# Pooled attention and a four-expert MLP on one core: queries by head pairs, low heads first, a new load order, and a re-ordered first chunk

## The chip, the cores and the metric

The kernel runs on one core of one Trainium2 chip. The metric is the device time of one execution in microseconds (us). The median of three runs of the kernel before is 489.83 us (489.71 to 490.68). One further execution was profiled; all rows below come from it.

The engines are named as in the profile: PE is TensorE (PEld its weight loads), DVE VectorE, ACT ScalarE, POOL GpSimd, SP SyncE. L12 is line 12 of the kernel before.

## The reference, cut to what matters

```
k_p = k.reshape(B, H, Sp, 8, D).mean(axis=3)      # B=8, H=8, S=576, D=64, Sp=72
v_p = v.reshape(B, H, Sp, 8, D).mean(axis=3)
attn = softmax(q @ k_p.T / sqrt(D));  x = attn @ v_p
x = x.transpose(0, 2, 1, 3).reshape(4608, 512)
p = domain_probs / domain_probs.sum(-1)
out = sum over e of p[:, e] * (relu(x @ w1[e]) @ w2[e])   # E=4, 512 -> 1024 -> 512
```

Attention over keys and values that are averaged eight by eight, then four experts of two layers, weighted by the given probabilities. Inputs and output are float32; the kernel computes in bfloat16 with float32 sums.

## The kernel before, in words

The 4608 tokens are worked on in nine chunks of 512: one for the first 512 tokens of each batch and one for the eight remainders of 64. A chunk and an expert are a step of the main loop. The two layers of an expert are not done as plain products but, in the main loop, in a seven-product scheme on half blocks (as in Strassen's method): `up_product` (L695) and `down` (L763) each make seven products per expert, with sums of weights (`weight_sums`, `first_weight_sums`), of inputs (`x_sum`) and of hidden values (`hidden_sums`), all by DVE at L246, in place of an eighth. `up` (L617), `up_quarter` (L631) and `down_plain` (L789) are plain products, used in the first chunk where the sums are not yet there.

All engines' orders are written out by hand (a manual schedule): the order of the calls is the order of the instructions on each engine, and semaphores are put in by the framework. So an instruction whose data is late holds everything behind it on its engine.

What the change touches:

- **The opening**, `attention_first`: batch 0's attention. `load_q` (L174) loads the queries as float32 in two halves of four heads, on SP's and ACT's queues; `round_q` (L186) casts a pair of heads to bfloat16 on DVE or ACT; `queries_first` (L364) turns a pair on PE and copies it back. Keys and values of batch 0 come by POOL's queue in four loads each (L142). They are pooled on PE: `choose_rows` and `rows_chosen` (L109, L110 on POOL and L246 on DVE) build a matrix of zeros and ones, `sum_keys` (L318) and `sum_values` (L306) multiply by it. `scores_first` (L545) with its exponential on ACT (L549), `context_quarter` (L440), the division on DVE (L429, L430) and `turn_quarter` (L455) follow for the low four heads (group 0) and the high four (group 1). `idle` (L338) issues matmuls on zeros: fillers, without a result that anyone reads.
- **The loads**: POOL's queue casts float32 to bfloat16 on the way. It brings, in the order of issue, batch 0's keys and values, the first layers of experts 0 to 2 with expert 0's second layer, expert 3's first layer, batch 1's keys (`load_whole`, L128, 72 partitions), batch 1's queries (L178), expert 1's second layer, batch 1's values in two loads, expert 2's second layer (`load_w2`, L216). Expert 3's second layer is issued from within `first_chunk`, since its buffer holds partial sums until then (`partial_first`).
- **The first chunk**, `first_chunk`: experts 0 to 3 on batch 0's tokens, with batch 1's attention in between. Here expert 0's and 1's first layers are plain; `both(e, step)` makes step `step` of the seven products for both units (halves of the hidden columns) of expert e. A unit has two PSUM banks. Step 0 fills bank 0, which ACT copies to bank 1 (L708); steps 2 and 3 add to bank 0, which ACT copies out after each (L710); step 1 and 6 add to bank 1, step 4 starts it anew and step 5 ends bank 0. ACT takes steps 1 and 5 (L712, L716), DVE steps 4 and 6 (L675). `down(c, e, step)` alternates between the two banks of `chains`; `down_plain(c, e, r)` uses `chains[r % 2]` for row block r, and its sum is added by DVE (L842). `fold_keys(1)` (L268, L286) and `values_folds(1)` (L268, L342) add up batch 1's eight rows on DVE; `queries_of_two` (L375, copy L378), `keys` (L297, copy L298), `scores_of_two` (L393), `context` (L467, L429, L430) and `turn` (L485, copy L486) are its attention.
- Behind `first_chunk` the **main loop** runs 7 x 32 slots, each with an up product of two units and a down step, and the next batch's pieces at planned slots. The change leaves it as it is.

The two functions that carry the order around the change are `attention_first` and `first_chunk`. The idle filler and the step that refills a bank, as written:

```
def idle(n, w_ps, cols=NT):
    for _ in range(n):
        nc.tensor.matmul(w_ps[:, 0:cols], lhsT=zeros[:, 0:P], rhs=zeros[:, 0:cols])
```

Of the kernel before, what the change touches and what calls it, by code (L numbers as in the profile page):

```python
# [17 lines left out]
def kernel(  # L18
# [10 lines left out]
    nc = tc.nc  # L29

    B, H, S, D = q.shape
    E, DM, F = moe_w1.shape
    P = nc.NUM_PARTITIONS
# [67 lines left out]

    ROWS = 9
# [96 lines left out]
    def load_w1(e):  # L199
        if e == 0:  # L200
            low, high = slice(0, HK), slice(HK, KC)
            parts = [(low, 0, 2), (high, 0, 2), (slice(0, KC), 2, 3), (slice(0, KC), 3, 4)]
        else:
            parts = [(slice(0, KC), 0, 4)] if e == E - 1 else [(slice(0, KC), 0, 2), (slice(0, KC), 2, 4)]
# [350 lines left out]
    def attention_first():  # L555
# [15 lines left out]
        sum_keys(0, (C0, C1))  # L571
        copy_keys(0, (C0, C1), (vector, scalar))
        idle(4, W2[:, 0], P)
# [21 lines left out]
        up_quarter(0, 1, (C0, C1))  # L595
        up_quarter(1, 1, (W2[:, 0], W2[:, 1]))
        for fc, bank in enumerate((B2[:, 0], A2[:, 0], C0, C1), HF):
            up(0, 0, (fc,), bank=bank)
# [274 lines left out]
    def first_chunk():  # L873
# [20 lines left out]
        each(sums[2][0], sums[2][1], sums[2][3], sums[2][2])  # L894
        up(0, 1, (5,), bank=chains[0])
        both(2, 0)
        up(0, 1, (6,), bank=chains[1])
        both(2, 1)
        up(0, 1, (7,), bank=chains[0])
        last_sum = weight_sums(0)  # L900
        each(sums[0][3], sums[1][3], *last_sum[0:2])
        both(2, 2)
        down(0, 0, 0)
        both(2, 3)
        hidden_sums(0, 0, 2)
        down(0, 0, 1)
        both(2, 4)
        hidden_sums(0, 0, 3)
        down(0, 0, 2)
        both(2, 5)  # L910
        each(*last_sum[2:])
        down(0, 0, 3)
        both(2, 6)
        each(*sums[3][0:2])
        both(3, 0)
        down(0, 0, 4)
        both(3, 1)
        each(sums[3][3], sums[3][2])
        fold_keys(1)
        down(0, 0, 5)  # L920
        both(3, 2)
        down(0, 0, 6)
        both(3, 3)
        queries_of_two(0, att[:, 0], nc.scalar.copy)
        both(3, 4)
        both(3, 5)
        keys(1, every)
        queries_of_two(2, chains[0][:], nc.scalar.copy)
        both(3, 6)
        load_w2(3)  # L930
        scores_of_two(1, 0, 0)
        down_plain(0, 1, 0)
        lo, hi = slice(0, H // 2), slice(H // 2, H)
        each(*values_folds(1, lo))
        scores_of_two(1, 2, 0)
        fold_first, *fold_rest = values_folds(1, hi)
        fold_first()
        down_plain(0, 1, 1)
        each(*fold_rest)
# [8 lines left out]
        down_plain(0, 1, 2)  # L948
        context(1, 0)
        down_plain(0, 1, 3)  # L950
# [3 lines left out]
        down_plain(0, 2, 0)  # L954
# [3 lines left out]
        down_plain(0, 2, 1)  # L958
# [3 lines left out]
        down_plain(0, 2, 2)  # L962
# [69 lines left out]
    with tc.manual_schedule(  # L1032
# [3 lines left out]
        load_first(k, "kraw", 1)  # L1036
        choose_rows()
        make_identity(nc, ident[:])
# [7 lines left out]
        rows_chosen(0)  # L1046
        rows_chosen(1)
# [79 lines left out]
```

## Time and profile before

| what | us |
|---|---|
| median of three runs | 489.83 |
| the profiled execution, own time | 489.93 |
| its span, first instruction to last | 488.2 |
| PE busy 0 to 6.4 / 6.4 to 17.7 | 4.90 / 10.17 |
| PE busy 17.7 to 50 (32.3 long) | 32.20 |
| PE busy 50 to 70.5 (20.5 long) | 19.87 |
| PE busy 70.5 to 488.2 (417.7 long) | 413.38 |
| ACT busy 50 to 70.5 | 8.46 |
| DVE busy 50 to 70.5 | 16.96 |
| busy share of the 16 DMA engines up to 70, in slices of 1.75 us | 0.9 or more in all but the first two |

How to read it: the span is what the trace covers; the execution's own time has 1.7 us around it. Busy PE counts pipelined matmuls whose ends are modelled, and they overlap, so a gap of 0.1 to 0.2 us between two matmuls does not show as idle. Whether PE lost time is read from the distance between the starts of neighbouring matmuls: eight 128x256 matmuls take 0.87 us in the chain, a 128x512 matmul 0.216 us from start to start, and anything above is a gap. For a group of instructions the timeline gives start, length and, in brackets, the idle time of the engine before it with what ended it.

### The profile page before, as it was taken

How to read it: one execution, taken by the hardware profiler on the slowest of the kernel's cores; microseconds unless marked ns; L12 is line 12 of the kernel's file. 1: busy time of each engine (PE TensorE's matmuls, PEld its weight loads, DVE VectorE, ACT ScalarE, POOL GpSimd, SP SyncE). 2: the span in 40 equal slices, each digit the busy share in tenths (PEclk: the TensorE clock that was granted, in tenths of full speed). 3: DMA queues.
4: the chain of work that ended last, by engine and by line, in shares of the span. 5: the costliest groups of instructions: out<-in, count | busy, mean ns of one | idle time of the engine just before them, and what ended most of it. 6: DMA issues, size and time to landing. Idle time of an engine off the chain costs nothing.

```text
span 488.2 us, 11522 instructions
## 1 busy us (share of the span) xinstructions
PE 480.5 (98%) x4673; PEld 409.4 (84%) x4678; DVE 376.9 (77%) x758; ACT 303.8 (62%) x576; POOL 119.4 (24%) x120
## 2 busy tenths in 40 slices
PE   8999999999999999999999999999999999999996
PEld 4669568898888888888888888888898888888885
DVE  4779799989768976798679866997678766876674
ACT  5677446855676567656765567556755567556650
POOL 8520504242523154016321442111011101010000
PEclk9999999999999999999999999999999999999999
DMA  9999999994986489345954298311111010004003
GB/s 195 203 209 203 204 170 155 103 90 54 110 110 63 77 86 137 35 83 56 159 50 91 27 165 66 68 23 66 35 23 23 23 64 3 12 23 87 1 1 87
DMA packets 104996, 41.96 MB, mean 86 GB/s; under 512 B 75504, under 2 KB 104432, under 8 KB 104944
## 3 DMA queue, kind: packets, MB, share of 16 engines
q0 software_dynamic: 58496, 22.35, 41.8%
q1 hardware_dynamic: 45328, 17.84, 16.7%
q10 hardware_dynamic: 1120, 1.05, 0.6%
q8 instruction: 36, 0.59, 0.5%
q14 instruction: 16, 0.13, 0.1%
HBM read 45.69 MB, written 9.44 MB: 113 GB/s over the span
## 4 chain that ended last, share of the span: by engine, by line
PE 91%; DMA 3%; ACT 2%; DVE 2%; POOL 1%; issue 1%; POOLq 0%; ACTq 0%
PE unit L695 42%; PE o_ps L763 41%; DMA w_bf<-in_moe_w_dram 3%; PE att L467 1%; PE unit L822 1%; PE o_ps L617 1%; PE att L393 1%; ACT expT L549 1%; PE unit L617 1%; PE unit L393 0%; DVE wt_bf L246 0%; POOL wt_bf L142 0%; ACT qT L378 0%; DVE acc L842 0%; PE work_first L631 0%
## 5 line engine op out<-in xcount | busy, mean ns | idle before, releaser
L842 DVE SCALAR_TENSOR_TENSOR acc<-o_ps,p_all,acc 128x256 f32<-128x256 f32 (+1 forms) x285 | 126.9, 485 | 52.9 <-PE o_ps L763 36.5
L763 PEld LDWEIGHTS <-H 128*128 128x128 bf16 x1320 | 129.1, 98 | 15.5 <-issue 0.6
L695 PEld LDWEIGHTS <-w_bf 128*128 128x128 bf16 x1088 | 105.2, 98 | 13.0 <-issue 0.2
L675 DVE CUSTOM_DVE_ANT_0 H<-unit,partial 128x512 bf16<-128x512 f32 x128 | 87.2, 684 | 23.8 <-ACT partial L710 11.5
L763 PE MATMUL o_ps<-w_bf,H 128*128 128x256 bf16 x792 | 102.6, 273 | 0.4 <-ACT o_ps L771 0.4
L695 PE MATMUL unit<-xT,w_bf 128*128 128x256 bf16 x704 | 100.5, 273 | 0.0
L777 POOL TENSOR_TENSOR acc<-acc,addend 128x512 f32<-128x512 f32 x24 | 30.7, 1279 | 253.2 <-ACT addend L775 202.2
L710 ACT COPY partial<-unit 128x512 f32<-128x512 f32 x128 | 72.3, 592 | 30.2 <-PE unit L695 30.2
L695 PEld LDWEIGHTS <-wu_bf 128*128 128x128 bf16 x816 | 77.6, 98 | 11.7 <-issue 2.5
L695 PE MATMUL unit<-xs,wu_bf 128*128 128x256 bf16 x512 | 77.0, 273 | 0.0
L763 PE MATMUL o_ps<-wt_bf,H 128*128 128x256 bf16 x528 | 68.4, 273 | 0.0
L712 ACT ACTIVATE H<-unit 128x512 bf16<-128x512 f32 x66 | 39.8, 605 | 30.9 <-PE unit L695 30.9
L763 PEld LDWEIGHTS <-S 128*128 128x128 bf16 x528 | 51.7, 98 | 6.0
L716 ACT ACTIVATE H<-unit 128x512 bf16<-128x512 f32 x66 | 39.6, 602 | 25.6 <-PE unit L695 25.3
L708 ACT COPY unit<-unit 128x512 f32<-128x512 f32 x68 | 39.4, 582 | 23.6 <-PE unit L695 18.0
L695 PE MATMUL unit<-xs,w_bf 128*128 128x256 bf16 x256 | 38.4, 273 | 0.0
L840 ACT ACTIVATE acc<-o_ps,p_all 128x256 f32<-128x256 f32 x72 | 30.7, 485 | 9.4 <-PE o_ps L763 7.7
L152 POOL DMA_DIRECT2D kraw<-in_k_dram x20 | 26.3, 1317 | 39.0 <-DMA kraw<-in_k_dram 39.0
L695 PE MATMUL unit<-xT,wu_bf 128*128 128x256 bf16 x240 | 35.7, 272 | 0.0
L763 PE MATMUL o_ps<-w_bf,S 128*128 128x256 bf16 x264 | 34.2, 273 | 0.0
L763 PE MATMUL o_ps<-wt_bf,S 128*128 128x256 bf16 x264 | 34.2, 273 | 0.0
L152 POOL DMA_DIRECT2D vraw<-in_v_dram x20 | 28.4, 1420 | 18.8 <-DMA vraw<-in_v_dram 18.5
(162 smaller groups left out, 500.2 us busy)
## 6 DMA issues: line engine op xcount, KB each, us to landing
out_dram<-acc SPq DMA_DIRECT2D x32, 256.0 KB, 4.2
w_bf<-in_moe_w_dram POOLq DMA_DIRECT2D x10, 512.0 KB, 17.4
q_sb<-in_q_dram POOLq DMA_DIRECT2D x7, 512.0 KB, 9.6
vraw<-in_v_dram POOLq DMA_DIRECT2D x22, 144.0 KB, 6.5
kraw<-in_k_dram POOLq DMA_DIRECT2D x21, 144.0 KB, 5.7
w_bf<-in_moe_w_dram POOLq DMA_DIRECT2D x2, 1024.0 KB, 17.8
w_bf<-in_moe_w_dram POOLq DMA_DIRECT2D x4, 256.0 KB, 7.3
wt_bf<-in_k_dram POOLq DMA_DIRECT2D x4, 144.0 KB, 5.4
```

What stands on the lines that cost most here:

```text
L152: nc.gpsimd.dma_start(out=raw[:], in_=rows_of(src, b, 2 * part, 2 * part + 2), accum_op=ALU.add if part else ALU.bypass)
L617: nc.tensor.matmul(out_ps, lhsT=w1_bf[:, e, kc, fc * P:(fc + 1) * P], rhs=xT[:, kc, at], start=(kc == 0), stop=(kc == KC - 1), skip_group_ ...
L675: nc.vector._custom_dve(TENSOR_ADD_SAT, out=dst, in0=ps, in1=part, s0=LARGEST, s1=0.0)
L695: nc.tensor.matmul(ps[:, n * HN:(n + 1) * HN], lhsT=lhs[:, kc, f:f + P], rhs=rhs[:, kc, :], start=(not grows and n == 0 and kc == 0), stop ...
L708: nc.scalar.copy(out=banks[1][:], in_=ps)
L710: nc.scalar.copy(out=part[:, step - 2], in_=ps)
L712: nc.scalar.activation(out=quarter(0, 0), in_=ps, func=ACT.Relu)
L716: nc.scalar.activation(out=quarter(0, 1), in_=ps, func=ACT.Relu)
L763: nc.tensor.matmul(ps[:, j], lhsT=lhs[:, i, j * P:(j + 1) * P], rhs=rhs[:, i, :], start=(not grows and i == 0 and j == 0), stop=(i == HF - 1),
L777: nc.gpsimd.tensor_add(out=dst, in0=dst, in1=addend[:])
L840: nc.scalar.activation(out=dst, in_=o_ps, func=ACT.Copy, scale=prob)
L842: nc.vector.scalar_tensor_tensor(out=dst, in0=o_ps, scalar=prob, in1=dst, op0=ALU.mult, op1=ALU.add,)
```

## The change

Queries of batch 0 are loaded in four loads of two heads, alternately on SP's and ACT's queues. The identity is built ahead of the row choice on POOL, and `rows_chosen` moves into `attention_first`. The opening's order changes: fillers 11 become 7 and are put differently (26 become 23 in all, of 512 or 128 columns); low keys are pooled ahead of the last query turn, the last turn's copy goes to DVE; both context quarters of the low heads come ahead of the second value pooling, and the last context quarter ahead of the first up product. Some results go to other PSUM banks.

`load_whole` splits the 72 partitions into 64 (in as many loads as before) and 8. `load_w1` cuts expert 1's first layer into a quarter, a quarter and a half of the hidden columns, and expert 2's by input rows (low half, high half) instead of by hidden columns. `load_w2(1)` moves ahead of batch 1's keys and queries.

In `first_chunk` the steps of expert 2 come earlier and closer together, expert 0's down steps follow with fewer products between them, expert 1's plain down products are cut into halves and start among expert 3's products, and batch 1's queries, keys, scores and contexts move behind expert 3's products.

```diff
@@ load_whole
+        rows = src[b].rearrange("h (j r) d -> j h r d", r=POOL)
         for i in range(n):
             hs = slice(i * H // n, (i + 1) * H // n)
-            nc.gpsimd.dma_start(
-                out=raw[:, hs], in_=src[b].rearrange("h (j r) d -> j h r d", r=POOL)[:, hs])
+            nc.gpsimd.dma_start(out=raw[0:EVEN, hs], in_=rows[0:EVEN, hs])
+        nc.gpsimd.dma_start(out=raw[EVEN:], in_=rows[EVEN:])
@@ load_q
-        for group, queue in enumerate((nc.sync, nc.scalar)):
-            hs = slice(4 * group, 4 * group + 4)
-            queue.dma_start(out=wide_q[:, hs], in_=src[:, hs])
+        for pair in range(NPAIR):
+            hs = slice(2 * pair, 2 * pair + 2)
+            (nc.sync, nc.scalar)[pair % 2].dma_start(out=wide_q[:, hs], in_=src[:, hs])
@@ load_w1
+            1: [(every, 0, 1), (every, 1, 2), (every, 2, 4)],
+            2: [(low, 0, 4), (high, 0, 4)],
@@ attention_first
-        idle(11, W2[:, 0])
+        idle(7, W2[:, 0])
         round_q(0, vector)
         round_q(1, scalar)
         queries_first((0,), C0, vector)
+        idle(1, W2[:, 0])
+        queries_first((1,), C1, scalar)
         round_q(2, vector)
         round_q(3, scalar)
-        idle(1, W2[:, 0])
-        queries_first((1,), C1, scalar)
-        idle(3, W2[:, 0], P)
+        rows_chosen(0)
+        rows_chosen(1)
         queries_first((2,), B2[:, 0], vector)
-        queries_first((3,), A2[:, 0], scalar)
-        idle(1, W2[:, 0])
-        sum_keys(0, (C0, C1))
-        copy_keys(0, (C0, C1), (vector, scalar))
-        idle(4, W2[:, 0], P)
+        idle(3, W2[:, 0])
+        sum_keys(0, (W2[:, 0], W2[:, 1]))
+        copy_keys(0, (W2[:, 0], W2[:, 1]), (vector, vector))
+        queries_first((3,), C1, vector)
+        idle(3, C0, P)
         scores_first(0, 0, B2)
         scores_first(0, 1, A2)
         sum_keys(1, (C0, C1))
         copy_keys(1, (C0, C1), (vector, vector))
-        idle(6, W2[:, 0], P)
+        idle(5, W2[:, 0], P)
         scores_first(1, 0, W2)
+        scores_first(1, 1, B2)
         sum_values(0, (C0, C1))
         cast_values(0, vector)
-        scores_first(1, 1, B2)
+        idle(4, A2[:, 0], P)
         context_quarter(0, 0, A2)
+        context_quarter(1, 0, W2)
         sum_values(1, (C0, C1))
         cast_values(1, scalar)
-        context_quarter(1, 0, W2)
         turn_quarter(0, 0, A2[:, 0], scalar)
         context_quarter(0, 1, B2)
-        turn_quarter(1, 0, W2[:, 0], scalar)
-        up_quarter(0, 0, (C0, C1))
-        context_quarter(1, 1, A2)
-        turn_quarter(0, 1, B2[:, 0], scalar)
-        up_quarter(1, 0, (W2[:, 0], W2[:, 1]))
-        turn_quarter(1, 1, A2[:, 0], vector)
+        turn_quarter(1, 0, C0, scalar)
+        context_quarter(1, 1, W2)
+        up_quarter(0, 0, (C1, A2[:, 0]))
+        turn_quarter(0, 1, C0, scalar)
+        up_quarter(1, 0, (B2[:, 0], B2[:, 1]))
+        turn_quarter(1, 1, W2[:, 0], vector)
...
@@ first_chunk, the new order from expert 1's up 5 on (the old one is in the listing above)
+        up(0, 1, (5,), bank=chains[0])
+        both(2, 0)
+        each(*sums[2][0:2], sums[2][3], sums[2][2])
+        up(0, 1, (6,), bank=chains[1])
+        up(0, 1, (7,), bank=chains[0])
+        both(2, 1)
+        both(2, 2)
+        last_sum = weight_sums(0)
+        each(sums[0][3], sums[1][3], last_sum[0])
+        both(2, 3)
+        down(0, 0, 0)
+        both(2, 4)
+        each(last_sum[1])
+        both(2, 5)
+        down(0, 0, 1)
+        hidden_sums(0, 0, 2)
+        both(2, 6)
+        down(0, 0, 2)
+        hidden_sums(0, 0, 3)
+        each(*last_sum[2:])
+        down(0, 0, 3)
+        down(0, 0, 4)
+        each(*sums[3][0:2])
+        both(3, 0)
+        down(0, 0, 5)
+        both(3, 1)
+        each(sums[3][3], sums[3][2])
+        down(0, 0, 6)
+        both(3, 2)
+        first, second = range(HF), range(HF, FCH)
+        down_plain(0, 1, 0, first)
+        both(3, 3)
+        down_plain(0, 1, 1, first)
+        both(3, 4)
+        down_plain(0, 1, 0, second)
+        fold_keys(1)
+        both(3, 5)
+        down_plain(0, 1, 1, second)
+        both(3, 6)
+        load_w2(3)
+        queries_of_two(0, att[:, 0], nc.scalar.copy)
+        queries_of_two(2, chains[1][:], nc.scalar.copy)
+        down_plain(0, 1, 2, first)
+        keys(1, every)
+        down_plain(0, 1, 2, second)
+        lo, hi = slice(0, H // 2), slice(H // 2, H)
+        each(*values_folds(1, lo))
+        scores_of_two(1, 0, 0)
+        down_plain(0, 1, 3)
+        each(*values_folds(1, hi))
+        scores_of_two(1, 2, 0)
+        down_plain(0, 2, 0, first)
+        down_plain(0, 2, 1, first)
...
         context(1, 0)
+        down_plain(0, 2, 0, second)
         context(1, 1)
         turn(1, 0)
         hidden_sums(0, 3, 0)
+        down_plain(0, 2, 1, second)
         context(1, 2)
         turn(1, 1)
         hidden_sums(0, 3, 1)
+        down_plain(0, 2, 2)
         context(1, 3)
         turn(1, 2)
         each(*weight_sums(3)[0:3])
-        down_plain(0, 2, 2)
         turn(1, 3)
         each(*(lambda n=n: x_sum(1, n) for n in range(3)))
@@ the opening calls
+        make_identity(nc, ident[:])
         choose_rows()
-        make_identity(nc, ident[:])
...
-        rows_chosen(0)
-        rows_chosen(1)
...
+        load_w2(1)
         load_whole(1, k, "kraw")
         load_q(1)
-        load_w2(1)
         load_whole(1, v, "vraw", 2)
```

More of the change, by code (lines that the diff above doesn't have):

```diff
@@ L99 @@
     raw_v = rawpool.tile([SP, H, 2, D], BF16, name="vraw")
+    EVEN = SP // 16 * 16
     ROWS = 9
@@ L199, in load_w1 @@
     def load_w1(e):
[L200 to L204, printed above, removed]
+        every, low, high = slice(0, KC), slice(0, HK), slice(HK, KC)
+        parts = {
+            0: [(low, 0, 2), (high, 0, 2), (every, 2, 3), (every, 3, 4)],
+            1: [(every, 0, 1), (every, 1, 2), (every, 2, 4)],
+            2: [(low, 0, 4), (high, 0, 4)],
+            3: [(every, 0, 4)],
+        }[e]
         for ks, lo, hi in parts:
@@ L577, in attention_first @@
         copy_keys(1, (C0, C1), (vector, vector))
-        idle(6, W2[:, 0], P)
+        idle(5, W2[:, 0], P)
         scores_first(1, 0, W2)
+        scores_first(1, 1, B2)
         sum_values(0, (C0, C1))
         cast_values(0, vector)
-        scores_first(1, 1, B2)
+        idle(4, A2[:, 0], P)
         context_quarter(0, 0, A2)
+        context_quarter(1, 0, W2)
         sum_values(1, (C0, C1))
         cast_values(1, scalar)
-        context_quarter(1, 0, W2)
         turn_quarter(0, 0, A2[:, 0], scalar)
         context_quarter(0, 1, B2)
-        turn_quarter(1, 0, W2[:, 0], scalar)
-        up_quarter(0, 0, (C0, C1))
-        context_quarter(1, 1, A2)
-        turn_quarter(0, 1, B2[:, 0], scalar)
-        up_quarter(1, 0, (W2[:, 0], W2[:, 1]))
-        turn_quarter(1, 1, A2[:, 0], vector)
-        up_quarter(0, 1, (C0, C1))
-        up_quarter(1, 1, (W2[:, 0], W2[:, 1]))
-        for fc, bank in enumerate((B2[:, 0], A2[:, 0], C0, C1), HF):
+        turn_quarter(1, 0, C0, scalar)
[4 more added lines that the diff above has]
+        turn_quarter(1, 1, W2[:, 0], vector)
+        up_quarter(0, 1, (C1, A2[:, 0]))
+        up_quarter(1, 1, (B2[:, 0], B2[:, 1]))
+        for fc, bank in enumerate((W2[:, 0], C0, C1, B2[:, 0]), HF):
             up(0, 0, (fc,), bank=bank)
@@ L893, in first_chunk @@
         up(0, 1, (4,), bank=units[0][1][:])
-        each(sums[2][0], sums[2][1], sums[2][3], sums[2][2])
         up(0, 1, (5,), bank=chains[0])
         both(2, 0)
+        each(*sums[2][0:2], sums[2][3], sums[2][2])
         up(0, 1, (6,), bank=chains[1])
+        up(0, 1, (7,), bank=chains[0])
         both(2, 1)
-        up(0, 1, (7,), bank=chains[0])
+        both(2, 2)
         last_sum = weight_sums(0)
-        each(sums[0][3], sums[1][3], *last_sum[0:2])
-        both(2, 2)
+        each(sums[0][3], sums[1][3], last_sum[0])
@@ L903, in first_chunk @@
+        both(2, 3)
         down(0, 0, 0)
-        both(2, 3)
+        both(2, 4)
+        each(last_sum[1])
+        both(2, 5)
+        down(0, 0, 1)
         hidden_sums(0, 0, 2)
-        down(0, 0, 1)
-        both(2, 4)
+        both(2, 6)
+        down(0, 0, 2)
         hidden_sums(0, 0, 3)
-        down(0, 0, 2)
-        both(2, 5)
         each(*last_sum[2:])
         down(0, 0, 3)
-        both(2, 6)
+        down(0, 0, 4)
         each(*sums[3][0:2])
         both(3, 0)
-        down(0, 0, 4)
+        down(0, 0, 5)
@@ L917, in first_chunk @@
         both(3, 1)
         each(sums[3][3], sums[3][2])
-        fold_keys(1)
[L920 to L925, printed above, removed]
+        down(0, 0, 6)
[6 more added lines that the diff above has]
+        down_plain(0, 1, 0, second)
+        fold_keys(1)
@@ L926, in first_chunk @@
         both(3, 5)
-        keys(1, every)
-        queries_of_two(2, chains[0][:], nc.scalar.copy)
+        down_plain(0, 1, 1, second)
         both(3, 6)
         load_w2(3)
-        scores_of_two(1, 0, 0)
-        down_plain(0, 1, 0)
+        queries_of_two(0, att[:, 0], nc.scalar.copy)
[3 more added lines that the diff above has]
+        down_plain(0, 1, 2, second)
         lo, hi = slice(0, H // 2), slice(H // 2, H)
@@ L934, in first_chunk @@
         each(*values_folds(1, lo))
+        scores_of_two(1, 0, 0)
+        down_plain(0, 1, 3)
+        each(*values_folds(1, hi))
         scores_of_two(1, 2, 0)
[L936 to L939, printed above, removed]
+        down_plain(0, 2, 0, first)
+        down_plain(0, 2, 1, first)
         load_wide(0, 0)
@@ L947, in first_chunk @@
         load_wide(1, 2)
-        down_plain(0, 1, 2)
         context(1, 0)
-        down_plain(0, 1, 3)
+        down_plain(0, 2, 0, second)
         context(1, 1)
@@ L953, in first_chunk @@
         hidden_sums(0, 3, 0)
-        down_plain(0, 2, 0)
+        down_plain(0, 2, 1, second)
         context(1, 2)
@@ L957, in first_chunk @@
         hidden_sums(0, 3, 1)
-        down_plain(0, 2, 1)
+        down_plain(0, 2, 2)
         context(1, 3)
```

## The prediction

> **What bounds the kernel now.** I read the page first, then the chain, the waits, and the timeline of the first 75 us. Times are us from the span's start; PE is TensorE, ACT ScalarE, DVE VectorE.
>
> ```profile
> PE 480.5 (98%) x4673; PEld 409.4 (84%) x4678; DVE 376.9 (77%) x758; ACT 303.8 (62%) x576; POOL 119.4 (24%) x120
> ...
> PE 91%; DMA 3%; ACT 2%; DVE 2%; POOL 1%; issue 1%; POOLq 0%; ACTq 0%
> ```
>
> PE does nearly all of the chain. The waits of PE from 65 us to the end are one line:
>
> ```profile
> PE o_ps L763 <- ACT o_ps L771: 0.4, 1, 0.4
> ```
>
> It falls at 70.53. Behind it PE issues at its row pace (eight 128x256 matmuls in 0.87, a 128x512 matmul in 0.216), so the end stands at a fixed distance from there, and the change counts by when PE gets there. The chain in order of time:
>
> ```profile
> 49.18 0.93 ACT qT L378
> ...
> 50.96 14.25 DMA w_bf<-in_moe_w_dram
> ...
> 65.23 0.70 DVE wt_bf L246
> ...
> 69.91 0.58 ACT o_ps L771
> ...
> 70.53 1.03 PE o_ps L763 x8
> ```
>
> Expert 3's second layer lands at 65.21; its sums hold DVE, DVE holds an add, the add holds ACT's copy, and PE waits. How much would an earlier landing be worth? Not 14.25 but PE's bubbles. Start to start beyond the row pace, PE loses 0.55 at 70.53, 0.19 at a context (56.48), some 0.45 around the score turns (49.5 to 52.7) and 0.2 in crumbs: **1.4** between its first plain up product (19.46, with the record missing ahead of L617's 19.68 put back) and 74.5. Ahead of that lies the opening:
>
> ```profile
> 1.25 4.87 PE L338 MATMUL work_first<-H 128*128 128x512 bf16 x11 [1.25 <-DVE H L863]
> ...
> 8.39 0.49 PE L318 MATMUL o_ps<-S,wt_bf 64*64 64x72 bf16 x36
> ...
> 12.71 0.69 PE L306 MATMUL o_ps<-wt_bf,S 64*72 64x128 bf16 x18
> ```
>
> Filler matmuls first, key pooling (L318) at 8.39 though the trace lands its second key load at 7.34, and the second value pooling (L306) at 12.71, its load landing at 12.41.
>
> **The opening, part by part.** Keys still leave POOL at 1.33 and values at 5.45 (identity and row choice swap places between them, same sum), so the landings 7.34, 8.74, 10.22, 12.41 and, for expert 0's weights, 13.94 to 18.37 stay. The queries' 1 MB is cut in four: the first pair should land near 4 instead of 5.51, and the casts, the row choice (two DVE subtractions, 0.50 each) and three query turns then fit ahead of 7.34. The fourth turn moves behind the pooling; it is needed only by the high heads. Pooling starts at 7.4, 1.0 earlier. Not all of it arrives: the last value load is fixed at 12.41, so that pooling gains only 0.26. Behind it before shows three PE gaps at turns, 0.28, 0.49 and 0.16, because the last context stood behind eight up products; it now stands ahead of them, and I find 0.5 of gaps left. With 0.1 from the casts the first plain up product comes **0.8 earlier**, near 18.7. Bounds: 0 (all pinned by 12.41) and 1.05 (the whole head start). I take 0.8, nearer the gaps that I can name. The three fillers fewer stand in waits and cost nothing.
>
> **The loads.** Batch 1's keys use 72 partitions: of the load's 16 completions in the trace, four come at 37.84 to 38.57 and twelve at 41.26 to 42.84, and every load behind inherits the spread. 64 + 8 rows remove most of it. A balanced 512 KB weight half takes 2.54 (31.21 to 33.77), so by that step: expert 1's second layer 41.3 and 43.9, keys 47, queries 50, values 52.5, expert 2's second layer 54.7 and 57.3. Expert 3's issue waits for the DVE result that frees its buffer (50.96 before, about 55.5 in the new order) and lands near 64.5. Laid out by the rows, their users come at 45.5, 50.7, 52.4, 57.8, 59.5 and 68.3. No load is late. The tightest is expert 2's first layer: its low rows land at 26.1, PE wants them at 27. The three small loads more cost POOL some 0.8 each, with nothing behind them in need. What this buys is the 1.4 of bubbles, no more; cover enough that a load 2 us later still costs nothing.
>
> **The new order of the first chunk.** PE's work is the same, so only waits count. I put the new order beside the rows, each instruction starting when its engine is free and its operands are there. These rows carry it:
>
> ```profile
> 35.81 1.29 DVE L675 CUSTOM_DVE_ANT_0 partial<-unit,w_bf 128x512 bf16<-128x512 f32 x2 [0.66 <-PE unit L695]
> 37.02 0.68 DVE L246 TENSOR_TENSOR H<-H,S 128x1024 bf16<-128x1024 bf16 x1
> 37.61 0.68 DVE L246 TENSOR_TENSOR wt_bf<-w_bf,wt_bf 128x1024 bf16<-128x1024 bf16 x1
> 38.22 0.68 DVE L246 TENSOR_TENSOR w_bf<-w_bf 128x1024 bf16<-128x1024 bf16 x1
> ...
> 43.71 1.93 DVE L268 TENSOR_TENSOR wt_bf<-wt_bf 72x2048 bf16<-72x2048 bf16 x2
> 45.68 0.76 DVE L286 TENSOR_TENSOR kp<-wt_bf 72x512 bf16<-72x512 bf16 x2
> ```
>
> 1. `both(2,1)`, `both(2,2)`, `both(2,3)` back to back. Step 3 refills the bank that step 2's copy empties. ACT must first take up 7 (0.49 to the next start), two of step 1 (0.99) and one of step 2 (0.59, and 0.05 to PE): 2.12 from up 7's result, where PE has two products, 1.74, less the 0.17 by which a result trails. **0.6.**
> 2. `down(0,0,4)` right behind `down(0,0,3)`. It reads w2's block that DVE rewrites last. The five instructions above run in just this order: 35.81 to 38.90 is 3.09, 0.08 of handing over. From the first one's start PE has one half product (0.44) and two down steps (1.75), less 0.17. Before, two more products (1.75) lay between. **1.15.**
> 3. The second query turn now writes `chains[1]`, so it waits for the add of `down_plain(0,1,1)`, and that add stands on DVE behind the key folds: add 0.66 + folds and keys 2.64 + add 0.75 + 0.05 = 4.1 from `down_plain(0,1,0)`'s result; PE has three products and eight transposes, 2.9. **1.2.** Then the keys' transposes wait in the same bank for the 1.04 copy: 1.3 with one half `down_plain` (0.87) beside it, **0.4.**
> 4. `turn(1,3)` follows `context(1,3)` with only `turn(1,2)` between; `down_plain(0,2,2)`, which lay there, now stands ahead.
>
> ```profile
> 62.97 0.75 DVE L842 SCALAR_TENSOR_TENSOR acc<-o_ps,p_all,acc 128x512 f32<-128x512 f32 x1
> 63.63 0.20 DVE L429 RECIPROCAL inv<-att 128x8 f32<-128x8 f32 x1
> 63.87 0.69 DVE L430 TENSOR_TENSOR x_tok<-att,inv 128x512 bf16<-128x512 f32 x1
> ```
>
> From that product's result DVE ends a sum (0.13), then add, reciprocal and division, 62.97 to 64.56, 1.6 and 0.05; PE has 0.3. **1.45.**
> 5. The same reckoning leaves 0.25 at the first `down_plain` half and 0.45 at two contexts. **0.7.**
>
> Together **5.5**. Bounds: 3.3, if items 1 to 4 are each 0.3 less and the small ones vanish; 6.5, if DVE's instructions overlap by 0.05 instead of the rows' 0.09.
>
> **Sum.** 489.93 (the profiled execution's own time, 0.10 above the median; its span is 488.2) - 0.8 - 1.4 + 5.5 = **493.2**.
>
> **The clock.** The first fillers start 0.43 apart (4.87 for eleven), later ones pass in 0.22: PE is at half pace until about 6.2. Four of those fillers go, so PE is less densely busy from 4.2 on. [...] Worked out from rows: if half pace lasted to about 9.5, then behind 7.4 the 36 key matmuls add 0.3, four transposes 0.2, three small fillers 0.15 and eight score matmuls 0.4, 1.1 in all, and nothing later absorbs it, since no load is awaited any more.
>
> **Rivals.**
> - *Late clock:* the above, 494.3. Against it: PE still has fillers between the turns. 20%.
> - *Opening pinned:* the head start is lost at 12.41 and the opening gains nothing: 494.0. The change then does not do what its first part says. For it: that load is fixed. Against: the gaps at 13.6 to 17.5. 8%.
> - *Engines hand over faster:* ACT and DVE start earlier than I reckon, e.g. on partial results, and the new waits come to 3.6 or so: 491.3. 12%.
> - *The loads decide (the other side):* the chain's one large foreign piece is the DMA. If PE's waits fall together because DVE, no longer held to 65.2, runs ahead of PE all along, the new waits shrink below 2.2 (0.8 + 1.4) and the kernel is faster; with 0.5 left, 488.2. For it: the 14.25 in the chain. Against: DVE is held by PE's results in items 2 to 4, not by loads. 5%.
> - *Forecast:* 493.2, 55%, from 492.3 to 494.0 by itself.
>
> The range 491.6 to 494.9 takes in the forecast, the late clock and the pinned opening, and leaves out the last rival and the edges. A measurement tells 0.2%, about 1 us, from no change. Faster by more: 0.05; within: 0.04; slower by more: 0.91, where all but one case lie.
>
> **What would show it.** In the profile after: key pooling at 7.4 to 7.6; the first plain up product near 18.7; PE waits on DVE ahead of the fifth down step of expert 0 and ahead of batch 1's second query turn, over 1 each; a wait on the division at batch 1's last turn, about 1.4; expert 3's second layer landing ahead of its use, and no DMA in the chain past 20 us. I am wrong if those waits are each under 0.5, or if filler matmuls still start 0.43 apart at 7 us (late clock).

## The result, and the profile after

The changed kernel takes **495.78 us** (median of four runs, 493.93 to 496.5), the kernel before 490.25 beside it (four runs, 489.71 to 491.0): ratio 1.0106, 95% interval 1.0074 to 1.0138. The forecast was 493.2 (491.6 to 494.9): slower is right, the size is not, 5.5 instead of 3.3. The profiled execution took 495.83, its span is 494.1.

The page of the kernel after, busy times and the shares of the chain of work that ended last:

```profile
PE 482.0 (98%) x4675; PEld 410.0 (83%) x4675; DVE 377.2 (76%) x760; ACT 303.6 (61%) x574; POOL 120.6 (24%) x123
...
PE 93%; DVE 4%; DMA 1%; ACT 1%; issue 0%; SPq 0%; DVEq 0%
```

PE has the same work; in its chain DMA fell from 3% to 1% and DVE rose from 2% to 4%. What PE waited for between 18 and 80 us (who <- for whom: total, times, longest):

```profile
PE unit L490 <- DVE x_tok L435: 1.3, 1, 1.3
PE o_ps L380 <- DVE acc L849: 1.1, 1, 1.1
PE o_ps L770 <- DVE w_bf L251: 1.0, 1, 1.0
PE unit L702 <- ACT w_bf L717: 0.4, 1, 0.4
PE o_ps L302 <- ACT qT L383: 0.2, 1, 0.2
PE att L472 <- DVE x_tok L435: 0.2, 1, 0.2
```

Line numbers of the changed kernel stand five to seven above those of before: L490 is the turn, L380 the query turn, L770 the down step, L702 the up product. Before had one line here, 0.4 for ACT; after has six, and none is a load. Read from start to start, beyond the row pace, they are 1.51 at the last turn, 1.25 at the second query turn, 1.17 at the fifth down step, 0.57 at the up products, 0.40 at the keys, 0.39 and 0.16 at two contexts, and 0.22 at the first plain down half: 5.67 in all. The large ones stand in the chain behind their releasers, for instance:

```profile
1.33 5.37 DMA acc<-in_q_dram
...
55.62 0.67 DVE acc L849
56.34 0.62 PE o_ps L380 x8
...
70.39 0.70 DVE x_tok L435
71.14 0.40 PE unit L490 x4
```

The only DMA in it is a load of queries, at the very start. The timeline of the opening shows what that did:

```profile
6.72 0.43 DVE L189 CAST q_sb<-acc 128x512 bf16<-128x512 f32 x1 [0.89 <-DMA acc<-in_q_dram]
...
7.21 0.61 PE L369 MATMUL att<-ident,q_sb 128*128 128x128 bf16 x4 [0.98 <-DVE q_sb L189]
7.61 1.48 PE L343 MATMUL work_first<-H 128*128 128x512 bf16 x3
...
9.03 0.75 PE L323 MATMUL work_first<-S,wt_bf 64*64 64x72 bf16 x36
```

The third pair's cast waits for its load until 6.72 and the turn until 7.21; behind it three fillers take 1.48, so they start 0.43 apart, and key pooling (L323) starts at 9.03. It was forecast for 7.4 to 7.6, and fillers 0.43 apart at 7 us are what the prediction names as the sign of a late clock.

For the account below I split each profiled execution at the start of its first plain up product and at the start of its last matmul. Where one 0.217 us matmul record is missing ahead of the first, it is put back.

| | before | after | difference |
|---|---|---|---|
| first plain up product | 19.46 | 20.48 | +1.02 (forecast -0.8) |
| from there to the last matmul ("interval") | 464.19 | 468.79 | +4.60 (forecast +4.1) |
| behind it, to the end of the execution | 6.28 | 6.56 | +0.28 |
| own time | 489.93 | 495.83 | +5.90 |

So the first chunk came out as forecast, within 0.5, and the opening 1.8 late.

### The profile page after: what moved, and what is told of

It reads as the page before. It is cut to its first block, busy times and chain, and to the rows that moved or that the text cites. A ratio compares the mean times of both kernels' runs of the same rounds, so it can differ in the third digit from the quotient of the medians.

```text
span 494.1 us, 11530 instructions
## 1 busy us (share of the span) xinstructions
PE 482.0 (98%) x4675; PEld 410.0 (83%) x4675; DVE 377.2 (76%) x760; ACT 303.6 (61%) x574; POOL 120.6 (24%) x123
## 4 chain that ended last, share of the span: by engine, by line
PE 93%; DVE 4%; DMA 1%; ACT 1%; issue 0%; SPq 0%; DVEq 0%
PE unit L702 41%; PE o_ps L770 40%; PE o_ps L796 2%; PE att L472 1%; PE unit L829 1%; DMA acc<-in_q_dram 1%; PE o_ps L624 1%; PE att L398 1%; DVE x_tok L435 1%; PE unit L624 1%; DVE acc L849 1%; PE unit L398 1%; DVE partial L682 0%; DVE wt_bf L273 0%; PE att L638 0%
## 5 line engine op out<-in xcount | busy, mean ns | idle before, releaser
L770 PEld LDWEIGHTS <-H 128*128 128x128 bf16 x1320 | 129.1, 98 | 15.0
L702 PEld LDWEIGHTS <-w_bf 128*128 128x128 bf16 x1088 | 105.2, 98 | 14.0 <-issue 0.8
L770 PE MATMUL o_ps<-w_bf,H 128*128 128x256 bf16 x792 | 102.6, 273 | 0.0
L702 PE MATMUL unit<-xT,w_bf 128*128 128x256 bf16 x704 | 100.4, 273 | 0.0
L702 PEld LDWEIGHTS <-wu_bf 128*128 128x128 bf16 x816 | 77.6, 98 | 11.9 <-issue 2.5
L702 PE MATMUL unit<-xs,wu_bf 128*128 128x256 bf16 x512 | 77.0, 273 | 0.0
L770 PE MATMUL o_ps<-wt_bf,H 128*128 128x256 bf16 x528 | 68.4, 273 | 0.0
L770 PEld LDWEIGHTS <-S 128*128 128x128 bf16 x528 | 51.6, 98 | 7.2 <-DVE w_bf L251 1.3
L702 PE MATMUL unit<-xs,w_bf 128*128 128x256 bf16 x256 | 38.4, 273 | 0.0
L702 PE MATMUL unit<-xT,wu_bf 128*128 128x256 bf16 x240 | 35.7, 272 | 0.0
L770 PE MATMUL o_ps<-w_bf,S 128*128 128x256 bf16 x264 | 34.2, 273 | 1.0 <-DVE w_bf L251 1.0
L770 PE MATMUL o_ps<-wt_bf,S 128*128 128x256 bf16 x264 | 34.2, 273 | 0.0
```

What stands on the lines that cost most here:

```text
L702: nc.tensor.matmul(ps[:, n * HN:(n + 1) * HN], lhsT=lhs[:, kc, f:f + P], rhs=rhs[:, kc, :], start=(not grows and n == 0 and kc == 0), stop ...
L770: nc.tensor.matmul(ps[:, j], lhsT=lhs[:, i, j * P:(j + 1) * P], rhs=rhs[:, i, :], start=(not grows and i == 0 and j == 0), stop=(i == HF - 1),
```

## The experiments

All results in one table. "Full clock" is when the trace's record of the granted clock first says full; ratios are to the kernel before, run beside it, with the 95% interval. Medians mix the opening, which varies from run to run (18.74 and 20.48 in two profiles of the same kernel), with the first chunk; so edits of the first chunk are judged by the interval.

| run | fillers at the start | full clock | first plain up product | interval | own time | median | ratio |
|---|---|---|---|---|---|---|---|
| before | 11 | 6.17 | 19.46 | 464.19 | 489.93 | 490.25 | |
| after | 7 | 10.49 | 20.48 | 468.79 | 495.83 | 495.78 | 1.0106 (1.0074 to 1.0138) |
| after_again | 7 | 4.77 | 18.74 | 468.79 | 494.05 | 495.20 | 1.0098 (1.0083 to 1.0114) |
| after_fillers | 11 | 4.31 | 18.68 | 468.79 | 494.02 | 494.40 | 1.0088 (1.0075 to 1.0102) |
| after_halves | 7 | 10.04 | 20.54 | 468.79 | 496.10 | 496.10 | 1.0119 (1.0101 to 1.0138) |
| before_short | 7 | 9.34 | 20.29 | 463.60 | 490.29 | 490.48 | 1.0017 (1.0008 to 1.0026) |
| open_only | 7 | 4.30 | 19.63 | 464.39 | 490.31 | 489.75 | 0.9995 (0.9986 to 1.0004) |
| chunk_only | 11 | 5.93 | 19.35 | 468.78 | 494.84 | 495.04 | 1.0103 (1.0089 to 1.0117) |
| even_only | 11 | 7.08 | 19.55 | 464.04 | 490.41 | 490.18 | 1.0004 (0.9996 to 1.0013) |
| down_fix | 7 | 5.15, lost to 11.98 | 21.08 | 467.91 | 495.57 | 494.64 | 1.0094 (1.0077 to 1.0110) |
| bank_fix | 7 | 4.98 | 18.73 | 468.41 | 493.73 | 493.69 | 1.0086 (1.0070 to 1.0103) |
| fold_fix | 7 | 4.65 | 19.01 | 468.01 | 493.54 | 493.91 | 1.0079 (1.0064 to 1.0093) |
| turn_fix | 7 | 6.05 | 18.50 | 468.88 | 493.94 | 494.39 | 1.0090 (1.0076 to 1.0104) |
| sums_turn | 7 | 4.10 | 18.58 | 468.46 | 493.72 | 495.27 | 1.0096 (1.0079 to 1.0113) |
| banks_apart | 7 | 5.67 | 19.27 | 468.75 | 494.53 | 494.24 | 1.0087 (1.0073 to 1.0101) |
| apart_sums | 7 | 6.34 | 19.49 | 468.10 | 494.08 | 493.95 | 1.0085 (1.0071 to 1.0099) |
| all_fix | 7 | 6.80 | 18.50 | 467.73 | 492.85 | 493.09 | 1.0070 (1.0055 to 1.0084) |
| best_chunk | 11 | 4.40 | 18.36 | 467.55 | 492.43 | 492.70 | 1.0058 (1.0046 to 1.0071) |
| best_after | 11 | 7.16 | 19.28 | 466.34 | 492.23 | 492.11 | 1.0045 (1.0031 to 1.0058) |
| before_best | 11 | 7.19 | 19.43 | 465.16 | 491.08 | 490.13 | 1.0008 (0.9999 to 1.0016) |

### Which part costs: open_only, chunk_only, even_only

```diff
 open_only = before
+load_q in four loads, attention_first, identity ahead of choose_rows, rows_chosen moved: as after
 chunk_only = after
+load_q, attention_first and the calls of the opening: as before
 even_only = before
+EVEN = SP // 16 * 16, load_whole in 64 + 8 partitions
```

> The kernel before with the new opening alone (queries in four loads, row choice and order of the opening); its loads behind the opening and its first chunk as before. Theory (the forecast failed in the opening, whose first plain up product came 1.0 later instead of 0.8 earlier): first plain up product at 20.2 to 20.8, clock released near 10.5 instead of 6.2, time 490.6 to 491.3, since the 1.0 is partly absorbed at the wait for expert 3's second layer, near 70 us. Rival (the opening is late only because the new order of loads disturbs it): first plain up product back near 19, time 489.5 to 490.2.

> The changed kernel with the opening of before: new order of loads and new order of the first chunk. Theory (the new waits of the first chunk are the 5.5 to 5.7 forecast, less 1.4 of bubbles): first plain up product near 19.5, 59.4 to 59.8 from it to the steady rows, time 494.2 to 495.0. Rival (the chunk costs more than forecast and the opening nothing): 495.5 or more.

> The kernel before with only the 64 + 8 split of the 72-partition loads of later batches. Theory (the spread of completions costs PE at most the wait at 70.5): completions of one load within 1.5 instead of 5, expert 3's second layer 0 to 2 earlier, time 489.6 to 490.3, no change. Rival (the spread is what holds the kernel): 489.0 or less.

The new first chunk with the old opening has the interval 468.78, 4.59 above before: the theory's. Its median, 495.04, stands 0.04 above the expected 495.0 and under the rival's 495.5. The new opening alone changes nothing that can be measured, 489.75 to 489.96, about one us less than I expected, and its clock came early (4.30), not late, so its profile does not show the late opening that it was meant to test. Its first plain up product still stands at 19.63, mostly because here PE waited 0.7 for expert 0's first weights. The split of the loads brings expert 3's second layer to 63.30 instead of 65.21 in its profile, and from batch 1's keys to that layer the sixteen completions of a load spread over 1.8 to 2.5 us instead of 4.0 to 5.7 (1.5 was expected). The time is the same, 490.18 to 489.96.

### The opening: after_again, after_fillers, after_halves, before_short

```diff
 after_again = after
 after_fillers = after
-        idle(7, W2[:, 0])
+        idle(11, W2[:, 0])
 after_halves = after
+load_q(0) in two halves, as before
 before_short = before
-        idle(11, W2[:, 0])
+        idle(7, W2[:, 0])
```

> The changed kernel once more, with nothing edited: how far do its own executions spread, and does the opening decide it? Theory (in some executions one of the sixteen completions of a second query load comes 1 to 2 later than the rest, PE then idles from 5.9 and the clock is granted late or taken back; in the others the opening is as forecast): the times spread from 493.5 to 496.5, and the profiled one follows its first plain up product at 475.2 to 475.5 plus that start, so 493.9 if it starts at 18.5 and 495.9 if at 20.5. Rival (the opening of the changed kernel is always late): all runs 495.5 to 496.5.

> The changed kernel with eleven fillers at the start instead of seven, so that PE is densely busy to about 6.1 as it was before. Theory (the clock is released late because PE is less densely busy from 4.4 on): granted clock full from about 6.2, fillers 0.22 apart behind it, first plain up product 19.0 to 19.6, time 494.3 to 495.0. Rival (the second pair of query loads, landing at 6.7 to 6.9, sets the opening, the clock nothing): first plain up product still 20.2 to 20.6, time 495.6 to 496.0.

> The changed kernel with the queries loaded in two halves again, everything else of the new opening kept. Theory (the second pair of loads brings the late completion): the halves land at 5.5 and 6.2 as before, no completion over 0.7 behind the others, first plain up product 18.8 to 19.5, times 494.0 to 494.8 with a spread under 1. Rival (late completions come with the new opening whatever the loads, or the first turn, now after 5.6, costs as much): 495.3 or more, or the same spread of over 2.

> The kernel before with seven fillers at the start instead of eleven, nothing else: PE stands idle from 4.2 until the first queries are turned, near 6.1, without any change in loads or order. Theory (the late clock comes from PE's idle stretch after too few fillers): clock granted at 8 to 10.5 in the profiled execution instead of 6.2, first plain up product 20.3 to 21.0 instead of 19.5, time 490.5 to 491.5. Rival (the clock is late for another reason, such as the four loads): first plain up product 19.4 to 19.7, time 489.7 to 490.2.

The changed kernel once more has the same interval to 0.01 and an opening 1.74 earlier; its times run from 494.05 to 495.6. Of its nine executions in both runs three lie at 493.9 to 494.4 and six at 495.2 to 496.5. The timeline of the early opening, for the rows shown above:

```profile
5.89 0.43 DVE L189 CAST q_sb<-acc 128x512 bf16<-128x512 f32 x1
...
6.38 0.40 PE L369 MATMUL att<-ident,q_sb 128*128 128x128 bf16 x4 [0.57 <-DVE q_sb L189]
6.61 0.81 PE L343 MATMUL work_first<-H 128*128 128x512 bf16 x3
...
7.86 0.48 PE L323 MATMUL work_first<-S,wt_bf 64*64 64x72 bf16 x35 [0.29 <-DMA wt_bf<-in_k_dram]
```

Two things differ. The third pair's turn starts at 6.38 instead of 7.21, since its load has landed: **0.83**. The three fillers take 0.81 instead of 1.48 and the pooling behind them 0.48 instead of 0.75, and from that turn to the first plain up product it is 12.36 instead of 13.27: **0.91**. Together they are the 1.74. The split holds for this pair: in the early execution 35 of the 36 key matmuls wait until 7.86 for the second key load, so with the clock in time a turn at 7.21 would have brought the pooling to 8.18 (0.97 behind the turn, as in the early execution), 0.3 late by these rows, which is an estimate. From the low heads' scores on (8.83 and 10.57) both executions take 9.91.

The load: in the late execution fifteen of the sixteen completions of SP's second query load come by 5.56 and the last at 6.70; in the early one they come by 5.74 and 5.87. Among fifteen profiles with four query loads the last completion is over 1 late in two, this one and down_fix (5.75 and 7.33).

The clock: seven fillers end at 4.4, and PE then does little until all queries are there. With eleven fillers the full clock came at 4.3 to 7.2 in all seven profiles of the table; with seven it came at 4.1 to 6.8 in nine of thirteen, and at 9.3 to 12.0 in four (down_fix is among the four, by its second grant at 11.98). down_fix shows it withdrawn, where PE stood idle for some 2 us ahead of its late load. Stages of 2 us: length, busy time of PE, PEld, DVE, ACT and POOL, then the granted clock, DMA share and GB/s:

```profile
6.00:8.00 2.00, 0.17 (x3) 0.17 (x4) 0.65 (x2) 0.89 (x2) 2.00 (x5) 1.00 1.21 205
8.00:10.00 2.00, 2.00 (x47) 1.20 (x45) 1.31 (x5) 0.16 (x1) 2.00 (x4) 0.64 1.19 196
10.00:12.00 2.00, 2.00 (x50) 1.26 (x48) 0.59 (x3) 0.81 (x1) 2.00 (x4) 0.51 1.23 181
12.00:14.00 2.00, 1.91 (x55) 1.56 (x44) 0.56 (x3) 2.00 (x3) 1.93 (x3) 1.00 1.43 198
```

PE is busy for 0.17 us of the first stage; in the second and third the clock is 0.64 and 0.51. The trace's record has it full from 5.15, half from 8.56, full from 11.98, two steps of 3.41. PE was not idle throughout the first of them: it was at work from 5.15 to 5.8 and from 7.83 to 8.56. The seven fillers take 3.17 at half pace, the eleven of before 4.87.

Counted by their columns (0.427 us for 512 at half pace, 0.216 at full), the matmuls fill 2.5 us or more of the 3.41 us that end with the first full clock, in all twenty profiles, and 2.5 or less of the 3.41 us before. In the late openings of after, after_halves and before_short that earlier stretch holds 1.8, 1.5 and 1.7. The count goes with the clock in these profiles; that it sets the clock is not shown. How these stretches lie against the fillers changes from execution to execution: with seven fillers the full clock came at 4.1 to 6.8 or at 9.3 to 12.0, so there the early clock is partly luck. In all_fix 1.2 of the 2.5 are query turns, without which 1.3 would be left, less than in those three.

after_fillers puts eleven back, and its four times lie at 494.02 to 494.63: none in the group above 495, where six of nine were. after_halves was expected to mend the opening and did not: its times run from 494.78 to 497.07. The halves land at 5.51 and 6.31 without a straggler, but PE stands idle from 4.4 to 6.11, the full clock comes at 10.04, and the first plain up product at 20.54, as late as in the profile of after:

```profile
6.11 0.61 PE L369 MATMUL o_ps<-ident,q_sb 128*128 128x128 bf16 x4 [1.68 <-DVE q_sb L189]
...
7.97 1.49 PE L343 MATMUL work_first<-H 128*128 128x512 bf16 x3
9.38 0.75 PE L323 MATMUL work_first<-S,wt_bf 64*64 64x72 bf16 x36
```

So the straggling load is one way to a late opening, and an idle PE with the clock still at half is another, without it. before_short confirms the second in the kernel before, where loads and order are untouched. Four fillers fewer, PE idle for 1.95 ahead of the first turn, the clock at 9.34, the first plain up product 0.83 later; yet the time is only 1.0017 (1.0008 to 1.0026), as its interval is 0.59 shorter. The old first chunk waits for loads, and takes up part of an opening that is late. In the new one PE waits for none: its interval is 468.78 to 468.79 for five openings from 18.68 to 20.54, and each us goes through.

### The waits of the first chunk, one at a time: down_fix, bank_fix, fold_fix, turn_fix

```diff
 down_fix
         down(0, 0, 3)
+        both(3, 0)
         down(0, 0, 4)
         each(*sums[3][0:2])
-        both(3, 0)
 bank_fix
-        queries_of_two(2, chains[1][:], nc.scalar.copy)
+        queries_of_two(2, att[:, 1], nc.scalar.copy)
 fold_fix
         down_plain(0, 1, 1, first)
+        fold_keys(1)
         both(3, 4)
         down_plain(0, 1, 0, second)
-        fold_keys(1)
 turn_fix
-        down_plain(0, 2, 2)
         context(1, 3)
         turn(1, 2)
         each(*weight_sums(3)[0:3])
+        down_plain(0, 2, 2)
         turn(1, 3)
```

> The changed kernel with step 0 of expert 3 (two products, 1.75) moved in between the fourth and the fifth down step of expert 0. Theory (forecast item 2: PE waits 1.15 for five DVE sums of weights): the wait ahead of the fifth down step falls to nothing, time 1.0 to 1.2 less than the changed kernel, 494.7. Rival (step 0's own sums or banks are not there yet and it waits instead): under 0.4 less.

> The changed kernel with batch 1's second query turn written to the other half of the attention's bank instead of the second chain's bank. Theory (forecast item 3: PE waits 1.2 for an add on DVE behind the key folds, because of the bank alone): no wait of over 0.2 ahead of the second query turn, at most 0.5 ahead of the keys' transposes, time 1.2 to 1.6 less than the changed kernel, 494.4. Rival (the wait moves to the next user of that bank, the plain down product of row 1's successor, or the keys' transposes): under 0.5 less.

> The changed kernel with the key folds of batch 1 issued ahead of expert 3's step 4 and nothing else; the second query turn still writes the second chain's bank. Theory (forecast item 3: PE waits 1.25 there for an add that stands behind the folds on DVE): that wait falls under 0.3, and the time from the first plain up product to the last matmul, 468.8 in the changed kernel, to 467.5 to 467.9. Rival (as with the other bank, where PE then waited 1.27 for ACT's copy of the first turn: another wait of the same length stands behind it): 468.4 or more.

> The changed kernel with the plain down product of expert 2, row 2, put back between the turn of piece 2 and the turn of piece 3 of batch 1's first attention. Theory (forecast item 4: PE waits 1.5 for the division): the wait ahead of the last turn falls from 1.5 to under 0.2, time 1.3 to 1.5 less than the changed kernel, 494.3. Rival (the slack is taken by the next wait or by DVE, which must do the same work anyway): under 0.5 less.

down_fix takes 0.88 off the interval, of 1.0 to 1.2 expected: the wait falls from 1.17 to 0.30. The order was the cause. bank_fix takes off 0.38 of the 1.2 to 1.6 that I expected. Of PE's waits there, the line of the second query turn:

```profile
PE att L380 <- ACT qT L383: 1.1, 1, 1.1
```

The add is no longer waited for, but now ACT's copy of the first turn is, which reads the same tile, `att`: 1.27 in place of 1.25. fold_fix leaves the bank and takes the folds out of the add's way: 0.78 off. The wait at the query turn is gone, and the keys, behind it, wait 0.87 instead of 0.40, again for that copy (the line among PE's waits):

```profile
PE o_ps L302 <- ACT qT L383: 0.7, 1, 0.7
```

So the add behind the folds was the cause, and a second cause stood 0.5 behind it. turn_fix gains nothing, 468.88. Its timeline:

```profile
65.41 0.75 DVE L849 SCALAR_TENSOR_TENSOR acc<-o_ps,p_all,acc 128x512 f32<-128x512 f32 x1
...
66.30 0.69 DVE L435 TENSOR_TENSOR x_tok<-att,inv 128x512 bf16<-128x512 f32 x1
...
67.05 0.42 PE L472 MATMUL att<-vp,expT 72*128 72x65 bf16 x8 [1.46 <-DVE x_tok L435]
```

The product no longer stands ahead of the last context, so this now waits, for the division of the context before it: 1.62 in place of 1.51.

### Why the last stretch holds: sums_turn, banks_apart, apart_sums

```diff
 sums_turn = turn_fix, and
         keys(1, every)
+        hidden_sums(0, 3, 0)
+        hidden_sums(0, 3, 1)
...
-        hidden_sums(0, 3, 0)
...
-        hidden_sums(0, 3, 1)
 banks_apart = after, and
-        context(1, 1)
+        context_apart(1, 1)    # each half of the heads in a bank of unit 0, two divisions
...
-        down_plain(0, 2, 2)
-        context(1, 3)
+        context_apart(1, 3)
+        down_plain(0, 2, 2)
 apart_sums = banks_apart with the early hidden sums of sums_turn, and one 252-column matmul more in each context_apart
```

> The changed kernel with the plain down product of expert 2, row 2, between the turns of pieces 2 and 3, as in the run that gained nothing, and with the two sums of expert 3's hidden values (0.68 each on DVE) issued ahead of the contexts, where DVE idles 1.9. Theory (from 62.5 on DVE works without a pause up to 74, so a wait taken from PE there only moves to the next context; it goes if DVE has 1.4 less to do there): the waits ahead of the last context and the last turn together fall from 1.6 to under 0.5, first plain up product to last matmul 467.4 to 467.8 instead of 468.8. Rival (the contexts wait for each other through the bank that they share, not for DVE's load): 468.5 or more.

> The changed kernel with batch 1's contexts 1 and 3 in the two banks of unit 0 instead of the attention's own two, each with its division in two halves, and the plain down product of row 2 between context 3 and the turn of piece 2. Theory (the contexts wait for each other's division through the bank that they share, and one product can't cover both that and the turn): the waits at contexts and turns, together 2.1 in the changed kernel, fall under 0.6, first plain up product to last matmul 467.0 to 467.5 instead of 468.8. Rival (DVE's load holds them, as it works there without a pause): 468.3 or more.

> The changed kernel with contexts 1 and 3 in unit 0's banks, the plain down product of row 2 between context 3 and the turn of piece 2, and the two sums of expert 3's hidden values ahead of the contexts: bank and load of DVE treated together, which gained nothing and 0.3 when treated apart. Theory (both hold the last stretch, so that only both together free it): waits at contexts and turns under 0.6 of 2.1, first plain up product to last matmul 467.0 to 467.6 instead of 468.8. Rival (DVE's divisions and additions alone fill that stretch): 468.2 or more.

banks_apart (and best_chunk below) leaves out the 252-column matmul that follows the contexts in unit 0's second bank in apart_sums and best_after; in these two, part of one sum of batch 1's chunk is missing. Otherwise PE's instructions are the same.

Less work for DVE alone takes 0.42 off turn_fix's interval (468.88 to 468.46, where 467.4 to 467.8 was expected), other banks alone 0.04 off that of after (468.75 for an expected 467.0 to 467.5). Both together take off 0.69, net of the two added matmuls (0.13 and 0.11 from start to start); expected were 1.2 to 1.8. In their place stands a third holder, the bank of the turns, which ACT empties; among PE's waits:

```profile
PE unit L511 <- ACT xT L512: 0.7, 1, 0.7
```

So neither theory was right alone. Three holders stand closely one behind another: the division through the shared bank, DVE's load, ACT's copy of the turn before.

### Adding up: all_fix, best_chunk, best_after, before_best

```diff
 all_fix = down_fix, bank_fix, fold_fix, turn_fix together, and
         up(0, 1, (6,), bank=chains[1])
-        up(0, 1, (7,), bank=chains[0])
         both(2, 1)
+        up(0, 1, (7,), bank=chains[0])
         both(2, 2)
 best_chunk = the same up product, down_fix, fold_fix, banks_apart, idle(11)
 best_after = best_chunk with the added matmul and the early hidden sums
 before_best = open_only with idle(11) and even_only
```

> The changed kernel with all the waits of the first chunk treated at once: the three edits above, the key folds ahead of expert 3's step 4, and one plain up product put between steps 1 and 2 of expert 2. Opening as changed. Theory (the new waits are worth their sum, 4.2 to 4.8 of 5.7): 491.0 to 491.6; the rest above the kernel before is the opening's 1.0. Rival (DVE is so full in the first chunk that the waits return elsewhere): 492.5 or more.

> The changed kernel with every edit that took a wait away: step 0 of expert 3 ahead of the fifth down step, an up product between steps 1 and 2 of expert 2, the key folds early, contexts in separate banks, eleven fillers. Theory (0.9, 0.3, 0.8 and 1.6 of waits gone, the clock safe): first plain up product to last matmul 465.2 to 465.8, first plain up product 18.6 to 19.0, time 490.4 to 491.3, so still not below the kernel before, whose interval is 464.2. Rival (as the edits move DVE's work together, a wait comes back elsewhere): 491.8 or more.

> That, with the three edits that took a wait away each (step 0 of expert 3 ahead of the fifth down step, an up product between steps 1 and 2 of expert 2, the key folds early) and eleven fillers. Theory (waits of 0.9, 0.3, 0.8 and 1.5 gone): first plain up product to last matmul 465.4 to 466.2, time 490.4 to 491.4, still above the kernel before, whose interval is 464.2. Rival (a wait comes back): 492 or more.

> First chunk and order of loads as before; the new opening with eleven fillers instead of seven, and the 64 + 8 split. Theory (an opening 0.7 ahead with a safe clock, and loads without the late four completions, each take a part of the bubbles of before): first plain up product 18.7 to 19.0, time 489.0 to 489.6. Rival (the queue of loads sets the pace of the first chunk of before, so that a head start runs into the next load): 489.7 to 490.2.

all_fix was expected to gain 4.2 to 4.8 and gained 1.06 of the interval: turn_fix's wait of 1.62 at the context and bank_fix's of 1.26 for ACT's copy both stand in it. best_chunk gained 1.24 of 3.0 to 3.6, best_after 2.45 of 2.6 to 3.4. What PE still waits for in best_after:

```profile
PE o_ps L302 <- ACT qT L383: 0.7, 1, 0.7
PE unit L511 <- ACT xT L512: 0.7, 1, 0.7
PE unit L723 <- ACT w_bf L738: 0.3, 1, 0.3
```

It is the best version of the changed kernel, 492.11, and still 1.0045 (1.0031 to 1.0058) of the kernel before. before_best did not become faster either: its clock came at 7.19, its first plain up product at 19.43, and PE waited 1.25 at a context near 58. No version tried beats the kernel before.

## Why the prediction was wrong, point by point

- **The loads**: right. PE awaits no load behind the opening. Expert 3's second layer lands at 67.1 instead of 64.5, but the first sum that reads it starts at 71.0. What that buys, the bubbles of before, is 5.67 - 4.60 = 1.07 by the account, where 1.4 was taken.
- **Item 1** (three steps back to back): 0.57 for 0.6. **Item 2** (fifth down step): 1.17 for 1.15. **Item 3** (second query turn, keys): 1.25 and 0.40 for 1.2 and 0.4. **Item 4** (last turn): 1.51 for 1.45. **Item 5**: 0.22 and 0.39 + 0.16 for 0.25 and 0.45. Together 5.67 for 5.5. The new order laid beside the rows of before told every wait with its place and releaser. The rival "engines hand over faster" is out, and so is "the loads decide": they needed new waits of 3.6 and of less than 2.2.
- **The opening**: the step that failed. "The first pair should land near 4 instead of 5.51, and the casts, the row choice (two DVE subtractions, 0.50 each) and three query turns then fit ahead of 7.34" holds in after_again: pair one lands at 4.39, the three turns are issued by 6.4, pooling begins at 7.35, the first plain up product comes at 18.74, forecast 18.7. One premise was off even there: the second key load landed at 7.82 instead of 7.34, so most of the pooling came at 7.86. That cost little, since the second value pooling is tied to its own load (12.55 instead of 12.71), and the rest of the 0.72 was gained behind it. The step fails in the profiled execution of after, where pair one lands at 4.14 but the third at 6.70. I reasoned from the first pair and took the others as given; the third turn waits for the third pair.
- **The clock**: "The three fillers fewer stand in waits and cost nothing" failed with it. I had named the late clock, priced it at 1.1 (it measures 0.91) and gave it 20%, against it "PE still has fillers between the turns". These stand behind the turns, and wait with them. The 9.5 to which that estimate lets half pace last stands in no row of before; the late openings showed the full clock at 9.34 (before_short), 10.04 (after_halves) and 10.49 (after). The rival's own sum, 494.3, lacked the late pair, 0.83, and shares what the forecast has too low in the account below, 0.85.
- **The account** closes. With the early opening: 489.93 - 0.72 + 4.60 + 0.24 (behind the last matmul, where the profiles lie anywhere between 6.28 and 6.82) = 494.05, inside the range and 0.85 above the forecast. With the late one: 494.05 + 1.74 + 0.04 = 495.83.
- **How often**: by their times six of nine executions of after are of the late kind, but only one of the six was profiled, and whether the others had a late load, a late clock or both is not known. Both came together in two of fifteen profiles with four query loads (after, down_fix). That the clock comes late without a late load, where PE is idle for 1.68 or 1.95 ahead of the first turn, is shown (after_halves, 10.04; before_short, 9.34). Why one completion of a load straggles is open; nothing tried touches it. Whether after_fillers avoids it or only its cost, four executions can't say.

## What to carry to other kernels

In a hand-written order, lay the new order beside the rows of the old profile, engine by engine: that gave the waits to 0.1 us a term. Then look at the start separately: where an opening hangs on the last of several loads and on when the full clock is granted, as here, its time can differ from one execution to the next, by 1.74 us between the two profiles of this kernel, and fillers that are placed behind a wait don't keep PE busy through it (2.03 idle in down_fix). A kernel that waits for loads later can forgive part of a late opening (0.59 of 0.83 in before_short); with those waits gone the opening counted in full (468.78 to 468.79 behind five openings).

A wait taken out is worth its length only if nothing else holds the same instruction: here five edits that aimed at 4.2 to 4.8 gained 1.1, since a bank, an engine's queue and a copy stood 0 to 0.5 behind one another.

## What the runs showed that was not expected

- The granted clock was lost again within the opening of down_fix: full at 5.15, half at 8.56, full at 11.98, with PE idle for 2.03 us up to 7.83.
- One of sixteen completions of a 256 KB load came 1.1 to 1.6 behind the other fifteen (5.56 and 6.70; 5.75 and 7.33), in two of fifteen profiles.
- The interval behind the opening repeats to 0.01 us (468.78 to 468.79) in five profiles with five openings, where PE awaits no load; with the first chunk of before, which waits for loads, it moves between 463.6 and 465.2.
